# Half steps ahead of the first outputs, single weight pieces and a reordered third tile in a fused attention and feed-forward kernel

## The chip, the cores and the metric

One core of one Trainium2 chip. The metric is the time of one execution on the device in microseconds (us). Runs of a kernel are called fast or slow: slow is a run more than 1.5% above the fastest of the same kernel. Kernels that are compared were run in turns on one chip, with the kernel before among them.

## The reference, cut to what matters

Lightning attention with a decaying state (4 batches, 8 heads, 768 positions, head width 64), then a gated feed-forward block over its 3072 tokens (width 512, inner width 1536).

```python
for b in range(nb):                               # 12 blocks of 64 positions
    intra = (einsum('bhic,bhjc->bhij', qb, kb) * Dmask) @ vb
    inter = (qb * lam_pow) @ kv_state
    out[:, :, sl] = intra + inter
    kv_state = lam_block * kv_state + (kb * rev_pow)^T @ vb
...
x = attn_out.transpose(0, 2, 1, 3).reshape(3072, 512)
g = x @ w_gate
out = (g * sigmoid(g) * (x @ w_val)) @ w_out
```

## The kernel before

The work is cut into 12 attention groups (two blocks of 128 positions each) and six feed-forward tiles of 512 tokens; tile t needs groups 2t and 2t+1. Everything is issued in one hand-made order: each `step(t, fc)` is one of the 12 slices of tile t's inner width (four gate and four value matmuls), and `at(step, fn, ...)` hangs other work behind a step.

Weights come as fp32 in pieces of one or two columns of 128, are cast to bf16 on ScalarE (gate) and GpSimd (value), and share raw buffers and SyncE's queue with q, k and v:

```python
def w_piece(c0, c1, eng=None):
    cs = slice(c0 * 128, c1 * 128)
    n = (c1 - c0) * 128
    if n == 128:
        both = raw_pool.tile([128, 2, MC, n], FP32, name="wraw", tag="raw")
    for j, (w_sb, w_d) in enumerate(((wg_sb, wg_d), (wv_sb, wv_d))):
        t = both[:, j] if n == 128 else raw_pool.tile([128, MC, n], FP32, name="wraw", tag="raw")
        (eng or nc.sync).dma_start(out=t, in_=w_d[:, :, cs])   # rows of n floats
        w_raw.append((w_sb[:, :, cs], t))
...
w_piece(0, 1); w_piece(1, 2); w_piece(2, 4); w_piece(4, 6)
```

A piece of two columns has rows of 1024 bytes in memory, a single one rows of 512. Groups from 3 on are transposed by a DMA, which `cast_scaled` issues behind its two casts; from group 6 on the casts are spread over the third tile (t = 2):

```python
def cast_scaled(g, eng=nc.vector):
    nc.scalar.copy(out=<k half of qk>, in_=kraw)
    eng.tensor_tensor(out=<q half of qk>, in0=qraw, in1=qfac(g), op=ALU.mult)
    dma_transpose(g)                              # on SyncE's queue
...
    at(s1b[11], ffn_out, 0, 0)                    # first output block
    at(s1b[11], ahead, 5)
    at(s1b[11], run_later, 3)
    at(s1b[11], ffn_out, 0, 1)
    at(s1b[11], core_a, 5)
    at(s1b[11], ffn_out, 0, 2)
    at(s1b[11], core_b, 5)
    at(s1b[11], cast_scaled, 6)                   # group 6's casts and transpose
    at(s1b[11], load_group, 7)
    at(s1b[11], v_scale, 6, nc.gpsimd)
    at(s1b[11], ffn_out, 0, 3)
```

Of the kernel before, what the change touches and what calls it, by code (L numbers as in the profile page):

```python
# [9 lines left out]
BF16 = mybir.dt.bfloat16  # L10
# [27 lines left out]
def _body(ctx, tc, nc, q, k, v, lam, moe_w_gate, moe_w_val, moe_w_out, out):  # L38
    B, H, S, D = q.shape
    HP = H // 2  # L40
    BLK = 128
# [3 lines left out]
    MC = DM // 128  # L45
    FC = DFF // 128
    NG = NBLK * B // 2
    M = BLK // 2
# [20 lines left out]
    xt_pool = ctx.enter_context(tc.tile_pool(name="xt", bufs=2))  # L69
    h_pool = ctx.enter_context(tc.tile_pool(name="h", bufs=2))  # L70
    sil_pool = ctx.enter_context(tc.tile_pool(name="sil", bufs=3))
# [7 lines left out]
    def bank():  # L79
        b = banks[ring[0] % 8]  # L80
        ring[0] += 1
        return b
# [44 lines left out]
    def warm_up(n, cols=512):  # L127
        b = bank()
        for _ in range(n):
            nc.tensor.matmul(b[:, 0:cols], warm[:, 0:128], warm[:, 0:cols], start=True, stop=True)  # L130
# [29 lines left out]

    lam_ps = bank()
    warm_up(4)
    nc.tensor.matmul(lam_ps[:, 0:H], ones[:, 0:128], lam_row, start=True, stop=True)
    warm_up(3)
    def warm_into(b, n, cols=256):
# [354 lines left out]
    def ffn_val(t, fc, b0=0, b1=B):  # L520
        if ("h", t) not in st:
            st[("h", t)] = h_pool.tile([128, FC, B, BLK], BF16, name="h", tag="h")
        h_sb, xt, sil = st[("h", t)], st[("xt", t)], st[("sil", t, fc, b0)]
        N = (b1 - b0) * BLK
        fs = slice(fc * 128, fc * 128 + 128)
        vp = bank()
        for mc in range(MC):
            nc.tensor.matmul(vp[:, 0:N], wv_sb[:, mc, fs],  # L528
                             xt[:, b0 // 2:b1 // 2, mc].rearrange("p g b n -> p g (b n)"),
                             start=(mc == 0), stop=(mc == MC - 1))  # L530
        nc.vector.tensor_tensor(out=h_sb[:, fc, b0:b1].rearrange("p b n -> p (b n)"),  # L531
                                in0=sil[:, 0:N], in1=vp[:, 0:N], op=ALU.mult)
# [5 lines left out]
    def ffn_out(t, b, last=False):  # L538
        h_sb = st[("h", t)]
        osb = osb_pool.tile([128, DM], FP32, name="osb", tag="osb")  # L540
        row = groups[2 * t + b // 2][0] * S + (groups[2 * t + b // 2][1] * 2 + b % 2) * BLK
        halves = ((0, DM // 2, nc.scalar.copy, nc.scalar), (DM // 2, DM, nc.vector.tensor_copy, nc.sync)) \
            if last else ((0, DM, nc.scalar.copy, nc.scalar),)
        for c0, c1, fn, eng in halves:
            ps = bank()[:, 0:c1 - c0]
            for fc in range(FC):
                nc.tensor.matmul(ps, h_sb[:, fc, b], wo_sb[:, fc, c0:c1],  # L547
                                 start=(fc == 0), stop=(fc == FC - 1))
            fn(out=osb[:, c0:c1], in_=ps)  # L549
            eng.dma_start(out=bass.AP(tensor=out.tensor, offset=out.offset + row * DM + c0,  # L550
                                      ap=[[DM, 128], [1, c1 - c0]]),
                          in_=osb[:, c0:c1])
# [25 lines left out]
    w_piece(1, 2)  # L578
    w_piece(2, 4)
    w_piece(4, 6)  # L580
    cast_half(0, 0, (None, DVEC))
# [79 lines left out]
    ring[0] = 2  # L661
    ffn_fc(0, 1, 2, 4)
    upd_copy(1, (1,))
    state(0)
# [17 lines left out]
    at(s0[3], load_group, 2, "kq")  # L682
    at(s0[3], w_piece, 10, 12)
    at(s0[3], swapped_q_table)
    at(s0[4], w_cast)
    at(s0[4], state, 1)
    at(s0[4], load_group, 2, "v")
    at(s0[5], load_group, 3)
# [6 lines left out]
    at(s0[8], w_cast)  # L695
    at(s0[8], v_scale, 2, nc.gpsimd)
    at(s0[9], scores, 2)
# [32 lines left out]
    at(s1b[6], wo_cast)  # L730
    at(s1b[6], v_scale, 5, nc.gpsimd)
    at(s1b[8], wo_cast)
    at(s1b[9], core_a, 4)
    at(s1b[10], core_b, 4)
    at(s1b[10], wo_cast, ACTC)
    at(s1b[11], ffn_out, 0, 0)
    at(s1b[11], ahead, 5)
    at(s1b[11], run_later, 3)
    at(s1b[11], ffn_out, 0, 1)
    at(s1b[11], core_a, 5)  # L740
    at(s1b[11], ffn_out, 0, 2)
    at(s1b[11], core_b, 5)
    at(s1b[11], cast_scaled, 6)
    at(s1b[11], load_group, 7)
    at(s1b[11], v_scale, 6, nc.gpsimd)
    at(s1b[11], ffn_out, 0, 3)

    outs = [(1, b) for b in range(4)]
    for t in range(2, NG // 2):
        sn = [step(t, fc) for fc in range(FC)]  # L750
        if t == 2:
            at(sn[2], ahead, 6)
        for j, g in ((3 if t == 2 else 0, 2 * t + 3), (7 if t == 2 else 6, 2 * t + 4)):
            if g < NG:
                at(sn[j], cast_scaled, g)
                if g + 1 < NG:
                    at(sn[j], load_group, g + 1)
                at(sn[1 + j], v_scale, g, nc.gpsimd)
        if t + 1 < NG // 2:
            at(sn[6 if t == 2 else 4], attend, 2 * t + 2)  # L760
            at(sn[10], attend, 2 * t + 3)
        for n, o in zip((0, 3, 7, 9), outs):
            at(sn[n], ffn_out, *o)
        outs = [(t, b) for b in range(4)]
# [41 lines left out]
```

## Time and profile before

| | kernel before |
|---|---|
| time, median of 3 | 228.36 us (228.12 to 229.23) |
| the profiled run | 229.38 us, 1.0 us above that median; span of the profile 227.7 us |
| TensorE busy | 218.2 us, 96% |
| largest wait of TensorE after 15 us | 1.77 us, first output block |

The columns are the stretch in us, its length, the busy time of each engine, the granted clock of TensorE, the mean busy share of the 16 DMA engines, and GB/s:

```profile
16.00:20.00 4.00, 4.00 (x41) 3.29 (x40) 1.82 (x5) 3.54 (x8) 1.81 (x4) 1.00 1.08 379
20.00:24.00 4.00, 4.00 (x20) 1.77 (x19) 1.54 (x3) 2.30 (x5) 3.11 (x7) 1.00 1.09 385
```

The transfer engines are full, and TensorE is full too. Both are at their limit at once. The timeline at 30 us (start, duration, engine, line, what) shows how close the two are:

```profile
30.48 1.18 POOL L273 CAST qk<-qraw 128x512 bf16<-128x512 f32 x2 [1.81 <-DMA qraw<-in_q_dram]
31.56 1.06 PE L289 MATMUL bank<-ident,qk 128*128 128x128 bf16 x16
```

GpSimd waits 1.81 us for group 2's q, casts it in two halves, and TensorE transposes it at 31.56 without a wait: there is no bracket on its line.

### The profile page before, as it was taken

What the parts mean: (1) busy time and instruction counts of PE and PEld (TensorE: products, weight loads), DVE (VectorE), ACT (ScalarE), POOL (GpSimd) and SP (SyncE); (2) the same over time, 40 slices, a digit from 0 to 9 for tenths busy, and PEclk for the clock granted to TensorE, in tenths of its full rate; (3) what the DMA queues carried; (4) which work ended last, traced back from release to release, by engine and by line L of the source; (5) the groups of instructions that cost most, each with busy time, mean ns of one, the idle gap of its engine ahead of it and who ended that gap; (6) DMA issues with size and microseconds to landing.
All of it is one profiled execution on the core that took longest, in us unless ns stands there. A gap on an engine that the chain in (4) does not pass through costs nothing.

```text
span 227.7 us, 5890 instructions
## 1 busy us (share of the span) xinstructions
PE 218.2 (96%) x2431; PEld 118.3 (52%) x2443; DVE 89.5 (39%) x151; ACT 107.2 (47%) x209; POOL 88.9 (39%) x131
## 2 busy tenths in 40 slices
PE   8789999999997999999999999999999999999994
PEld 3556456878853544454544544544544444444443
DVE  2664347685924213545362361353242123222200
ACT  5878585745562446464354363454433423322221
POOL 5676737641595232978373092092160000000000
PEclk9999999999999999999999999999999999999999
DMA  6999999899997879799877748815101101101122
GB/s 201 345 359 382 366 330 325 206 240 285 389 191 179 238 157 217 183 207 192 217 177 184 183 101 200 214 49 138 49 3 48 46 3 46 46 0 46 49 92 92
DMA packets 88012, 39.70 MB, mean 174 GB/s; under 512 B 57650, under 2 KB 83506, under 8 KB 87986
## 3 DMA queue, kind: packets, MB, share of 16 engines
q1 hardware_dynamic: 83474, 32.64, 55.3%
q10 hardware_dynamic: 4512, 6.69, 8.3%
q8 instruction: 19, 0.31, 0.6%
q14 instruction: 7, 0.06, 0.1%
HBM read 28.31 MB, written 6.29 MB: 152 GB/s over the span
## 4 chain that ended last, share of the span: by engine, by line
PE 82%; DMA 5%; SPq 5%; POOL 5%; issue 1%; ACT 0%; DVE 0%; DVEq 0%; POOLq 0%
PE bank L547 26%; PE bank L514 25%; PE bank L528 24%; SPq L99 4%; DMA woraw<-in_moe_w_out_dram 3%; DMA v<-in_v_dram 2%; POOL wo_sb L232 2%; POOL v_s L238 2%; PE bank L474 2%; PE bank L461 2%; PE bank L382 1%; PE bank L352 1%; SPq L227 1%; POOL kvf L421 1%; PE bank L326 0%
## 5 line engine op out<-in xcount | busy, mean ns | idle before, releaser
L531 DVE TENSOR_TENSOR h<-sil,bank 128x512 bf16<-128x512 bf16 (+1 forms) x87 | 51.5, 595 | 108.9 <-PE bank L528 93.2
L514 PE MATMUL bank<-xt,wg_sb 128*128 128x512 bf16 (+1 forms) x348 | 76.6, 343 | 0.0
L528 PE MATMUL bank<-xt,wv_sb 128*128 128x512 bf16 (+1 forms) x348 | 76.4, 342 | 0.0
L547 PE MATMUL bank<-wo_sb,h 128*128 128x512 bf16 (+1 forms) x288 | 64.3, 370 | 2.5 <-POOL wo_sb L232 1.8
L518 ACT ACTIVATE sil<-bank 128x512 bf16<-128x512 f32 (+1 forms) x87 | 45.8, 527 | 44.2 <-PE bank L514 41.2
L528 PEld LDWEIGHTS <-wv_sb 128*128 128x128 bf16 x348 | 34.0, 98 | 28.3
L547 PEld LDWEIGHTS <-h 128*128 128x128 bf16 x300 | 29.1, 98 | 34.3 <-issue 2.0
L514 PEld LDWEIGHTS <-wg_sb 128*128 128x128 bf16 x348 | 32.4, 98 | 27.2 <-DVE xt L486 0.3
L549 ACT COPY osb<-bank 128x512 f32<-128x512 f32 (+1 forms) x24 | 13.9, 578 | 55.4 <-PE bank L547 53.3
L238 POOL TENSOR_TENSOR v_s<-v,dec 128x1024 bf16<-128x1024 f32 (+1 forms) x14 | 23.2, 1667 | 14.4 <-DMA v<-in_v_dram 11.4
L421 POOL TENSOR_TENSOR kvf<-kvs,ups 128x256 f32<-128x256 f32 x8 | 5.8, 727 | 43.5 <-ACT ups L404 42.2
L333 DVE TENSOR_TENSOR ssb<-bank,causal 128x512 bf16<-128x512 f32 x24 | 15.3, 684 | 4.2 <-PE bank L326 4.1
L486 ACT CAST xt<-bank 128x512 bf16<-128x512 f32 x21 | 12.7, 663 | 2.9 <-PE bank L474 2.4
L421 POOL TENSOR_TENSOR kvf<-kvf,ups 128x256 f32<-128x256 f32 x16 | 13.4, 840 | 0.6
L430 POOL CAST kvn<-kvf 64x256 bf16<-64x256 f32 x24 | 11.6, 483 | 1.5
L404 ACT COPY ups<-bank 128x256 f32<-128x256 f32 (+1 forms) x24 | 9.5, 449 | 2.4 <-PE bank L382 1.4
L260 DVE TENSOR_TENSOR qk<-qraw,qdn 128x1024 bf16<-128x1024 f32 x6 | 7.7, 1280 | 4.5 <-DMA qraw<-in_q_dram 4.5
L258 ACT CAST qk<-kraw 128x1024 bf16<-128x1024 f32 x9 | 9.4, 1043 | 0.0
L357 DVE TENSOR_TENSOR ssb<-bank,causaln 128x512 bf16<-128x512 f32 x12 | 8.3, 688 | 1.2 <-PE bank L352 1.1
L232 POOL CAST wo_sb<-woraw 128x1024 bf16<-128x1024 f32 x5 | 5.1, 1040 | 7.3 <-DMA woraw<-in_moe_w_out_dram 7.3
L221 POOL CAST wv_sb<-wraw 128x1024 bf16<-128x1024 f32 (+1 forms) x6 | 5.8, 971 | 5.3 <-DMA wraw<-in_moe_w_val_dram 5.2
L474 PE MATMUL bank<-ssb,v_s 64*64 64x128 bf16 (+1 forms) x384 | 6.9, 208 | 0.5 <-ACT guard L445 0.5
(63 smaller groups left out, 117.2 us busy)
## 6 DMA issues: line engine op xcount, KB each, us to landing
out_dram<-osb ACTq DMA_DIRECT2D x23, 256.0 KB, 2.1
v<-in_v_dram SPq DMA_DIRECT2D x16, 256.0 KB, 4.7
woraw<-in_moe_w_out_dram SPq DMA_DIRECT2D x6, 512.0 KB, 7.4
kraw<-in_k_dram SPq DMA_DIRECT2D x24, 128.0 KB, 3.3
qraw<-in_q_dram SPq DMA_DIRECT2D x24, 128.0 KB, 3.6
wraw<-in_moe_w_gate_dram SPq DMA_DIRECT2D x5, 512.0 KB, 6.8
wraw<-in_moe_w_val_dram SPq DMA_DIRECT2D x5, 512.0 KB, 6.7
kraw<-in_k_dram SPq DMA_DIRECT2D x4, 512.0 KB, 6.9
```

Source lines behind the costliest of these rows:

```text
L238: eng.tensor_tensor(out=st[("vs", g)][:, h0:h1], in0=st[("v", g)][:, h0:h1].rearrange("p h (s d) -> p h s d", s=2), in1=vfac(g, h0, h1), o ...
L333: nc.vector.tensor_tensor(out=ssb[:, h2, 2 * c:2 * c + 2].rearrange("p a s n -> p a (s n)"), in0=sp[(c, h2)].rearrange("p (a x) -> p a x", ...
L421: nc.gpsimd.tensor_tensor(out=o, in0=f, in1=u, op=ALU.add)
L430: nc.gpsimd.tensor_copy(out=o[64 - h2 * 64:128 - h2 * 64], in_=f[h2 * 64:h2 * 64 + 64])
L474: nc.tensor.matmul(op[r][h2 * 64:h2 * 64 + 64, cols(g, hp, s)], v_s[ps, 2 * hp + h2, s], ssb[ps, h2, hp * 2 + s] if g >= NAT0 else ssb[ps, ...
L486: fns[r](out=xt[:, g % 2, :, r].rearrange("p h (m s) -> p h s m", s=2) if g < NAT0 else xt[:, g % 2, :, :, r * M:r * M + M], in_=op[r].rea ...
L514: nc.tensor.matmul(gp[:, 0:N], wg_sb[:, mc, fs], xt[:, b0 // 2:b1 // 2, mc].rearrange("p g b n -> p g (b n)"), start=(mc == 0), stop=(mc = ...
L518: nc.scalar.activation(sil[:, 0:N], gp[:, 0:N], AF.Silu)
L528: nc.tensor.matmul(vp[:, 0:N], wv_sb[:, mc, fs], xt[:, b0 // 2:b1 // 2, mc].rearrange("p g b n -> p g (b n)"), start=(mc == 0), stop=(mc = ...
L531: nc.vector.tensor_tensor(out=h_sb[:, fc, b0:b1].rearrange("p b n -> p (b n)"), in0=sil[:, 0:N], in1=vp[:, 0:N], op=ALU.mult)
L547: nc.tensor.matmul(ps, h_sb[:, fc, b], wo_sb[:, fc, c0:c1], start=(fc == 0), stop=(fc == FC - 1))
L549: fn(out=osb[:, c0:c1], in_=ps)
```

## The change: its intent, and the diff

The intent is to fill TensorE's one wait in the middle by running four half steps (a step over half of the tile's tokens, matmuls of 256 columns) of the third tile ahead of the first output block, with the casts of the output weights reordered; to get the first weights and group 2's v in smaller pieces, so that each can start sooner; to keep the start busy a little longer; and to take group 7's v from GpSimd to VectorE.

```diff
-    h_pool = ctx.enter_context(tc.tile_pool(name="h", bufs=2))
+    h_pool = ctx.enter_context(tc.tile_pool(name="h", bufs=5))    # halves of 6 slices
...
+    b = bank()
+    for n in range(30):
+        r = slice(n % 2 * 64, n % 2 * 64 + 64)
+        nc.tensor.matmul(b[r, 0:8], warm[r, 0:64], warm[r, 0:8], start=True, stop=True, skip_group_check=True)
+    warm_up(2)
+    nc.tensor.matmul(lam_ps[:, 0:H], ones[:, 0:128], lam_row, start=True, stop=True)
     warm_up(4)
-    nc.tensor.matmul(lam_ps[:, 0:H], ones[:, 0:128], lam_row, start=True, stop=True)
-    warm_up(3)
...
-        halves = ((0, DM // 2, ...), (DM // 2, DM, ...)) if last else ...
+        halves = ((0, DM - 128, ...), (DM - 128, DM, ...)) if last else ...
...
-    w_piece(2, 4)
-    w_piece(4, 6)
+    for c in range(2, 6):
+        w_piece(c, c + 1)
...
-    at(s0[3], w_piece, 10, 12)
+    at(s0[3], w_cast)
+    at(s0[3], w_piece, 10, 11)
...
-    at(s0[4], load_group, 2, "v")
+    at(s0[4], load_fp32, 2, nc.sync, v, "v", 0, H // 2)
+    at(s0[4], load_fp32, 2, nc.sync, v, "v", H // 2, H)
+    at(s0[4], w_piece, 11, 12)
...
-    at(s1b[6], v_scale, 5, nc.gpsimd)
     at(s1b[8], wo_cast)
+    at(s1b[8], v_scale, 5, nc.gpsimd)
     at(s1b[9], core_a, 4)
-    at(s1b[10], core_b, 4)
+    at(s1b[10], core_b, 4, SPLIT)
     at(s1b[10], wo_cast, ACTC)
-    at(s1b[11], ffn_out, 0, 0)
...
+    NH = 4
+    s2 = [step(2, fc, 0, 2) for fc in range(NH)][-1]
+    at(s2, ffn_out, 0, 0)
...                                               # the same order as before, behind s2
-        sn = [step(t, fc) for fc in range(FC)]
+        sn = [step(t, fc, 2 if t == 2 and fc < NH else 0) for fc in range(FC)]
...
-                at(sn[1 + j], v_scale, g, nc.gpsimd)
+                at(sn[1 + j], v_scale, g, nc.vector if g == 7 else nc.gpsimd)
```

More of the change, by code (lines that the diff above doesn't have):

```diff
@@ L46, in _body @@
     FC = DFF // 128
+    FH = FC // 2
     NG = NBLK * B // 2
@@ L520, in ffn_val @@
     def ffn_val(t, fc, b0=0, b1=B):
-        if ("h", t) not in st:
-            st[("h", t)] = h_pool.tile([128, FC, B, BLK], BF16, name="h", tag="h")
-        h_sb, xt, sil = st[("h", t)], st[("xt", t)], st[("sil", t, fc, b0)]
+        hn = ("h", t, fc // FH)
+        if hn not in st:
+            st[hn] = h_pool.tile([128, FH, B, BLK], BF16, name="h", tag="h")
+        h_sb, xt, sil = st[hn], st[("xt", t)], st[("sil", t, fc, b0)]
         N = (b1 - b0) * BLK
@@ L530, in ffn_val @@
                              start=(mc == 0), stop=(mc == MC - 1))
-        nc.vector.tensor_tensor(out=h_sb[:, fc, b0:b1].rearrange("p b n -> p (b n)"),
+        nc.vector.tensor_tensor(out=h_sb[:, fc % FH, b0:b1].rearrange("p b n -> p (b n)"),
                                 in0=sil[:, 0:N], in1=vp[:, 0:N], op=ALU.mult)
@@ L538, in ffn_out @@
     def ffn_out(t, b, last=False):
-        h_sb = st[("h", t)]
         osb = osb_pool.tile([128, DM], FP32, name="osb", tag="osb")
         row = groups[2 * t + b // 2][0] * S + (groups[2 * t + b // 2][1] * 2 + b % 2) * BLK
-        halves = ((0, DM // 2, nc.scalar.copy, nc.scalar), (DM // 2, DM, nc.vector.tensor_copy, nc.sync)) \
+        halves = ((0, DM - 128, nc.scalar.copy, nc.scalar), (DM - 128, DM, nc.vector.tensor_copy, nc.sync)) \
             if last else ((0, DM, nc.scalar.copy, nc.scalar),)
@@ L546, in ffn_out @@
             for fc in range(FC):
-                nc.tensor.matmul(ps, h_sb[:, fc, b], wo_sb[:, fc, c0:c1],
+                nc.tensor.matmul(ps, st[("h", t, fc // FH)][:, fc % FH, b], wo_sb[:, fc, c0:c1],
                                  start=(fc == 0), stop=(fc == FC - 1))
@@ L662, in _body @@
     ffn_fc(0, 1, 2, 4)
+    w_cast()
     upd_copy(1, (1,))
@@ L695, in _body @@
     at(s0[8], w_cast)
-    at(s0[8], v_scale, 2, nc.gpsimd)
+    at(s0[8], v_scale, 2, nc.gpsimd, 0, H // 2)
+    at(s0[8], v_scale, 2, nc.gpsimd, H // 2, H)
+    at(s0[9], w_cast)
     at(s0[9], scores, 2)
@@ L730, in _body @@
     at(s1b[6], wo_cast)
-    at(s1b[6], v_scale, 5, nc.gpsimd)
     at(s1b[8], wo_cast)
+    at(s1b[8], v_scale, 5, nc.gpsimd)
     at(s1b[9], core_a, 4)
-    at(s1b[10], core_b, 4)
+    at(s1b[10], core_b, 4, SPLIT)
     at(s1b[10], wo_cast, ACTC)
-    at(s1b[11], ffn_out, 0, 0)
-    at(s1b[11], ahead, 5)
-    at(s1b[11], run_later, 3)
-    at(s1b[11], ffn_out, 0, 1)
-    at(s1b[11], core_a, 5)
-    at(s1b[11], ffn_out, 0, 2)
-    at(s1b[11], core_b, 5)
-    at(s1b[11], cast_scaled, 6)
-    at(s1b[11], load_group, 7)
-    at(s1b[11], v_scale, 6, nc.gpsimd)
-    at(s1b[11], ffn_out, 0, 3)
+    NH = 4
+    s2 = [step(2, fc, 0, 2) for fc in range(NH)][-1]
+    at(s2, ffn_out, 0, 0)
+    at(s2, ahead, 5)
+    at(s2, run_later, 3)
+    at(s2, ffn_out, 0, 1)
+    at(s2, core_a, 5)
+    at(s2, ffn_out, 0, 2)
+    at(s2, core_b, 5)
+    at(s2, cast_scaled, 6)
+    at(s2, load_group, 7)
+    at(s2, v_scale, 6, nc.gpsimd)
+    at(s2, ffn_out, 0, 3)
     outs = [(1, b) for b in range(4)]
     for t in range(2, NG // 2):
-        sn = [step(t, fc) for fc in range(FC)]
+        sn = [step(t, fc, 2 if t == 2 and fc < NH else 0) for fc in range(FC)]
         if t == 2:
-            at(sn[2], ahead, 6)
-        for j, g in ((3 if t == 2 else 0, 2 * t + 3), (7 if t == 2 else 6, 2 * t + 4)):
+            at(sn[4], ahead, 6)
+        for j, g in ((4 if t == 2 else 0, 2 * t + 3), (8 if t == 2 else 6, 2 * t + 4)):
             if g < NG:
@@ L757, in _body @@
                     at(sn[j], load_group, g + 1)
-                at(sn[1 + j], v_scale, g, nc.gpsimd)
+                at(sn[1 + j], v_scale, g, nc.vector if g == 7 else nc.gpsimd)
         if t + 1 < NG // 2:
-            at(sn[6 if t == 2 else 4], attend, 2 * t + 2)
+            at(sn[7 if t == 2 else 4], attend, 2 * t + 2)
             at(sn[10], attend, 2 * t + 3)
-        for n, o in zip((0, 3, 7, 9), outs):
+        for n, o in zip((1, 5, 7, 9) if t == 2 else (0, 3, 7, 9), outs):
             at(sn[n], ffn_out, *o)
```

## The prediction

> **What bounds the kernel now**
>
> I read the busy shares first, then the chain of work that ended last, then the timeline around every idle gap of the TensorE that a listing by engine shows, and last the DMA issues.
>
> ```profile
> PE 218.2 (96%) x2431; PEld 118.3 (52%) x2443; DVE 89.5 (39%) x151; ACT 107.2 (47%) x209; POOL 88.9 (39%) x131
> PE   8789999999997999999999999999999999999994
> PE 82%; DMA 5%; SPq 5%; POOL 5%; issue 1%; ACT 0%; DVE 0%; DVEq 0%; POOLq 0%
> ```
>
> TensorE is the bound: 96% busy, and 82% of the chain is its own work. The row of 40 slices shows where it is not full: the first three slices (to 17 us, the first loads), the thirteenth (68 to 74 us), and the last. From 15 us to the end of the matmuls at 224.3 us a change can only take away idle time of TensorE; moving matmuls about is worth nothing in itself. The timeline of TensorE alone marks the idle time before each entry; from 15 us on it has three gaps of 0.16 to 0.27 us and this one:
>
> ```profile
> 69.57 1.02 PE L547 MATMUL bank<-wo_sb,h 128*128 128x512 bf16 x4 [1.77 <-POOL wo_sb L232]
> ```
>
> The chain of waits shows what made it:
>
> ```profile
> 61.70 0.70 POOL kvf L421
> 62.85 0.70 POOL kvf L421
> 63.62 0.61 POOL kvs L424
> 64.69 1.97 POOL wo_sb L232 x2
> 66.66 1.87 POOL v_s L238
> 68.54 0.99 POOL wo_sb L232
> 69.57 1.02 PE bank L547 x4
> ```
>
> The first output block (line 547) needs all twelve chunks (128 rows each) of the output weights. GpSimd casts chunks 4 to 7, then spends 1.87 us scaling group 5's v, and only then casts chunks 8 and 9. TensorE has done eight of its twelve matmuls by 67.8 us and waits until 69.57. Chunks 10 and 11, cast on ScalarE, were ready at 67.9.
>
> Two waits that cost nothing now lie close behind it:
>
> ```profile
> 80.66 1.80 SPq L251 DMA_TRANSPOSE qkt<-qk  x1
> 92.22 1.32 DVE L260 TENSOR_TENSOR qk<-qraw,qdn 128x1024 bf16<-128x1024 f32 x1
> 93.69 2.03 SPq L251 DMA_TRANSPOSE qkt<-qk  x1
> 96.96 1.92 POOL L238 TENSOR_TENSOR v_s<-v,dec 128x1024 bf16<-128x1024 f32 x1
> 98.93 0.44 PE L382 MATMUL bank<-v_s,qk 64*64 64x64 bf16 x32
> 99.20 0.50 PE L352 MATMUL bank<-qkt 64*64 64x64 bf16 x32
> ```
>
> These belong to groups 6 and 7. Group 6's transpose is issued at 80.66, group 7's loads stand behind it in SyncE's queue, group 7's q lands at 92.0, VectorE scales it, group 7's transpose goes out at 93.69 and takes 4.9 us to land, at 98.6. Its first reader (line 352) runs at 99.20: 0.6 us of slack. GpSimd's scaling of group 7's v ends at 98.88, 0.05 us before its reader (line 382). So the third tile is already fed just in time.
>
> **What the Trainium skill says**
>
> "TensorE: Matmul & The Clock Gate", section "Back-to-back issue gap", puts a warm matmul at N/2.4 + 2.5 ns, so 216 ns for 512 columns and 109 ns for 256. The trace agrees: in the chain twelve matmuls of 512 columns take 2.59 us (216 each), four of 512 take 0.86, four of 256 take 0.44. Halving a step therefore costs almost nothing.
>
> "GPSIMD Engine Reference", section "Elementwise — side-by-side cycle accounting", has a two-input operation about 1.96 times slower on GpSimd. Here the ratio is smaller, 1914 ns (v, line 238) against 1280 ns (q, line 260, the same shape on VectorE): 1.5.
>
> "SBUF — State Buffer", section "SBUF: two separate sides", says that a VectorE operation with two SBUF inputs and a GpSimd operation hold their shared port pair exclusively, and the later one blocks. The trace agrees: the GpSimd add that begins at 92.42, beside VectorE's q scaling, takes 1.70 us where its neighbours take 0.72.
>
> **The change part by part**
>
> 1. Half steps of the third tile (tile 2) ahead of the first outputs, with five half-size h buffers. Four half steps, each 4 gate and 4 value matmuls of 256 columns, 2 x 0.436 = 0.87 us: 3.49 us of work that comes before the first output block instead of after it. They need only group 4's x. Splitting its two evacuations over VectorE and ScalarE makes it ready at about 65.9 instead of 66.5, when the last half step of tile 1 ends (65.9). TensorE then reaches the first output block at 69.4. The cast order changes too: three weight casts before v, so chunks 8 and 9 are ready at 64.63 + 3 x 1.02 = 67.7. The wait is thus removed from both sides: the casts come earlier and TensorE comes later. Sum: -1.77. The halving adds some 0.01 us per group, 16 groups: +0.15. The fifth h buffer lets the half steps be written before the outputs release tile 0's.
>
> 2. The delay this makes. Group 5's attention, which stands between the output blocks, now comes 3.49 - 1.77 = 1.7 us later. ScalarE evacuates it and only then casts group 6's k, so group 6's transpose goes out at about 82.4 instead of 80.66. Group 7's loads follow it in the same queue: q lands at about 93.7, VectorE is done at 95.0, the transpose goes out at 95.2 and lands, with 4.5 to 4.9 us, at 99.7 to 100.1. TensorE's place for its reader: before the attention of group 6 the change puts eight steps instead of seven (+1.73) and removes 1.77 of wait, so still at about 99.2. That is a new wait of 0.5 to 0.9 us. Group 8 inherits the delay: its transpose landed at 110.4, reader at about 112.8, slack 2.4 us. There TensorE is 1.7 us earlier less the new wait, the transpose about 1.5 later: from -0.1 to +0.3. Sum, an estimate: +0.7.
>
> 3. Group 7's v on VectorE, 1.28 us instead of 1.92 on GpSimd. Its state additions on GpSimd begin 1.7 us later (they follow group 6's update), would end at about 98.7, and v behind them at 100.6: TensorE would have waited 1.5 us at line 382. On VectorE it can begin when it lands (about 95.4) and after the mask before it, 96.5, and ends by 97.8, ahead of 98.9. So this part gains nothing against the kernel before; it prevents a loss that part 1 would make. VectorE delays two products of h by about 2 us, which eight banks and three buffers for the gate absorb. Sum: 0.
>
> 4. Weight columns 0 to 5 in single pieces, group 2's v in halves ahead of column 11. No TensorE gap between 15 and 38 us is over 0.25 us, so nothing waits there for weights; two GpSimd casts of 617 ns replace one of 1042. Group 2's v scaling ended at 36.68, its reader began at 36.73: that wait is 0.1 us, and with attention's small gaps around it gives -0.1 to -0.2. Sum: -0.1.
>
> 5. Start: 30 tiny matmuls and two warm-ups before the decay row, instead of four warm-ups. Four took 1.86 us; thirty at 15 to 40 ns plus two is 1.3 to 2.0. ScalarE's logarithm began at 3.27 and its table load ended at 3.12, so at most 0.15 us. What bounds the start is the loads, group 1's v landing at 11.3, which do not change. Sum: -0.05.
>
> 6. Tail: the last block split 384 and 128 instead of 256 and 256. TensorE's sum is the same, 12 x (162 + 56) against 24 x 109. VectorE's copy shrinks from 424 ns (256 columns) towards 290, by the slope from 688 ns at 512; the last transfer halves to 64 KB. Sum: -0.2.
>
> Together: -1.77 + 0.15 + 0.7 - 0.1 - 0.05 - 0.2 = -1.27, so 227.1 us. I shade this to 226.9, because the positions of attention and casts in tile 2 look chosen to keep part 2's wait small, and my landing times move in a block where they might compress.
>
> **The rivals**
>
> (a) No new wait: the loads behind group 6's transpose catch up, and the whole 1.77 stays. For it: DMA moved only 9 GB/s at 80 to 82 us, so the queue is empty when the transpose goes out. Against it: the eight loads have 0.65 us each of issue time, serial, and that does not shrink. It gives 226.2.
>
> (b) The wait only moves: group 7's late transpose plus group 8's take back all of the 1.77. For it: every station of that chain is just in time, and loads of 64 by 64 pieces took 8 to 9 us from first issue to last landing. Against it: 0.6 and 2.4 us of slack must first be used up. It gives 228.0 to 228.4.
>
> (c) VectorE becomes the bound around 92 to 98 us: q, v and four masks of 0.69 us stand ahead of h products there, and its two-input operations block GpSimd's state additions, about 1 us each. If group 6's last state part comes after 98.6, TensorE waits. By my count it is ready at 96.8, or 97.8 with one more block: close. It would add up to 1 us, 227.9.
>
> **Range and chances**
>
> The sure part is -1.77 - 0.2 + 0.15 = -1.8, the uncertain part 0 to 1.7 of waits given back, and 0.2 each way for the rest. That makes 225.9 to 228.2 the range that should hold it 8 times in 10, with 226.9 as the prediction. 2% is 4.6 us; no idle time of that size exists after 15 us, and nothing above adds that much. So 0.03 faster, 0.95 within 2%, 0.02 slower.
>
> **What would show it right or wrong**
>
> Right: the gap before line 547's first block is gone and no GpSimd entry stands in the chain at 61 to 69 us; group 6's transpose is issued at 82 or later; a TensorE wait of 0.3 to 1 us stands before line 352's or its successor's scores of group 7, ended by the transpose; VectorE's v scaling ends before the update of group 7; the last copy takes about 0.3 us. Wrong: a gap remains at the first outputs (then ScalarE's cast or bank reuse holds the half steps), the start shifts by over 0.3 us, or TensorE waits for VectorE or GpSimd in tile 2 instead of the transpose.

## The result, and the profile after

| | before | after |
|---|---|---|
| time, median of 5 | 228.36 us | 231.71 us (230.24 to 236.39) |
| ratio of fast runs | | 1.0115, 95% interval 1.0065 to 1.0164 |
| span of the profile | 227.7 us | 228.5 us |

The kernel got slower by about 1%, where the prediction said 0.6% faster: still within 2%, but outside of its range. One of the five runs was slow (236.39 us, clock 0.985). Ratios are the mean time of one kernel's fast runs over that of the other's of the same rounds, so not quite the ratio of the medians quoted.

Busy time of the engines and the chain that ended last, after:

```profile
PE 220.5 (96%) x2504; PEld 121.8 (53%) x2504; DVE 92.0 (40%) x157; ACT 107.9 (47%) x215; POOL 88.6 (39%) x134
PE 79%; DMA 9%; SPq 7%; DVE 1%; issue 1%; POOL 0%; ACT 0%; DVEq 0%
```

POOL has left the chain, as meant, but the share of the transfers and of SyncE's queue went up from 5% and 5% to 9% and 7%. The list of TensorE's waits says where (line, what it waited for, total us, times, longest):

```profile
PE bank L294 <- POOL qk L278: 0.9, 1, 0.9
PE bank L519 <- ACT wg_sb L226: 0.5, 1, 0.5
PE bank L357 <- DMA qkt<-qk: 0.5, 1, 0.5
PE bank L534 <- POOL wv_sb L226: 0.4, 1, 0.4
```

The wait for the output weights is gone. Four took its place, three of them for weights and for group 2's q, before 34 us. Their origin is in the transfers of the start:

```profile
16.00:20.00 4.00, 4.00 (x37) 3.18 (x34) 1.63 (x4) 3.28 (x9) 1.54 (x4) 1.00 0.98 280
20.00:24.00 4.00, 4.00 (x20) 1.79 (x19) 1.38 (x2) 2.95 (x7) 2.79 (x5) 1.00 0.99 282
```

280 GB/s in place of 380, with the 16 engines still 98% busy: they aren't idle, they get less done. (The share counts overlapping packets, so it can pass 1.) Group 2's q lands at 32.8 us in place of 30.4, and the cast that began at 30.48 begins at 32.88:

```profile
32.88 0.62 POOL L278 CAST qk<-qraw 128x512 bf16<-128x512 f32 x1 [1.94 <-DMA qraw<-in_q_dram]
33.55 0.62 PE L294 MATMUL bank<-ident,qk 128*128 128x128 bf16 x8 [0.94 <-POOL qk L278]
```

In the third tile, group 6's and 7's transposes go out later than before (80.66 and 93.69 there), and TensorE waits for group 7's, as the prediction said:

```profile
84.66 1.92 SPq L256 DMA_TRANSPOSE qkt<-qk  x1
97.26 1.62 SPq L256 DMA_TRANSPOSE qkt<-qk  x1
102.15 0.45 PE L357 MATMUL bank<-qkt 64*64 64x64 bf16 x32 [0.47 <-DMA qkt<-qk]
```

### The profile page after: what moved, and what is told of

It is laid out like the page before. It is cut to its first block, busy times and chain, and to the rows that moved or that the text cites.

```text
span 228.5 us, 6054 instructions
## 1 busy us (share of the span) xinstructions
PE 220.5 (96%) x2504; PEld 121.8 (53%) x2504; DVE 92.0 (40%) x157; ACT 107.9 (47%) x215; POOL 88.6 (39%) x134
## 4 chain that ended last, share of the span: by engine, by line
PE 79%; DMA 9%; SPq 7%; DVE 1%; issue 1%; POOL 0%; ACT 0%; DVEq 0%
PE bank L552 26%; PE bank L519 23%; PE bank L534 23%; SPq L218 4%; DMA qraw<-in_q_dram 4%; SPq L100 3%; DMA wraw<-in_moe_w_val_dram 2%; DMA qkt<-qk 2%; PE bank L479 2%; PE bank L466 2%; PE bank L387 1%; DVE ssb L338 1%; PE bank L331 1%; DMA out_dram<-osb 1%; PE bank L357 1%
## 5 line engine op out<-in xcount | busy, mean ns | idle before, releaser
L523 ACT ACTIVATE sil<-bank 128x512 bf16<-128x512 f32 (+1 forms) x91 | 46.2, 511 | 41.4 <-PE bank L519 38.9
L552 PE MATMUL bank<-wo_sb,h 128*128 128x512 bf16 (+2 forms) x300 | 65.7, 371 | 0.0
L534 PEld LDWEIGHTS <-wv_sb 128*128 128x128 bf16 x364 | 35.4, 98 | 27.5 <-POOL wv_sb L226 0.9
L519 PEld LDWEIGHTS <-wg_sb 128*128 128x128 bf16 x364 | 33.8, 98 | 27.0 <-ACT wg_sb L226 1.0
L552 PEld LDWEIGHTS <-h 128*128 128x128 bf16 x300 | 28.6, 98 | 32.5
L243 POOL TENSOR_TENSOR v_s<-v,dec 128x1024 bf16<-128x1024 f32 (+1 forms) x14 | 21.5, 1544 | 16.8 <-DMA v<-in_v_dram 13.8
L491 ACT CAST xt<-bank 128x512 bf16<-128x512 f32 x20 | 12.2, 659 | 3.1 <-PE bank L479 2.7
L426 POOL TENSOR_TENSOR kvf<-kvf,ups 128x256 f32<-128x256 f32 x16 | 12.5, 778 | 0.6
L226 POOL CAST wv_sb<-wraw 128x512 bf16<-128x512 f32 (+1 forms) x9 | 6.4, 711 | 6.1 <-DMA wraw<-in_moe_w_val_dram 6.0
```

Source lines behind the costliest of these rows:

```text
L243: eng.tensor_tensor(out=st[("vs", g)][:, h0:h1], in0=st[("v", g)][:, h0:h1].rearrange("p h (s d) -> p h s d", s=2), in1=vfac(g, h0, h1), o ...
L426: nc.gpsimd.tensor_tensor(out=o, in0=f, in1=u, op=ALU.add)
L491: fns[r](out=xt[:, g % 2, :, r].rearrange("p h (m s) -> p h s m", s=2) if g < NAT0 else xt[:, g % 2, :, :, r * M:r * M + M], in_=op[r].rea ...
L519: nc.tensor.matmul(gp[:, 0:N], wg_sb[:, mc, fs], xt[:, b0 // 2:b1 // 2, mc].rearrange("p g b n -> p g (b n)"), start=(mc == 0), stop=(mc = ...
L523: nc.scalar.activation(sil[:, 0:N], gp[:, 0:N], AF.Silu)
L534: nc.tensor.matmul(vp[:, 0:N], wv_sb[:, mc, fs], xt[:, b0 // 2:b1 // 2, mc].rearrange("p g b n -> p g (b n)"), start=(mc == 0), stop=(mc = ...
```

## The experiments

The expectations use letters. P: single pieces are fetched more slowly. W, in the first four: the new start lets TensorE's clock rise later or fall back (in `e8_cast6_early`, W is another rival). W2: the longer start makes TensorE fetch its instructions earlier, and a stall of SyncE's issue comes with that. L: the first-output wait of the kernel before took up lateness from the start, which the changed kernel pays in full. T: the third tile's waits come from group 6's casts standing too late. C: such waits let TensorE's clock fall to half for a while. Rivals are told with each.

### One part at a time

The first four undo or do the two parts at the start. `e1_pieces_back` is the changed kernel with pairs and a whole v of group 2 again; `e2_only_pieces` is the kernel before with these pieces alone:

```diff
-    w_piece(2, 4)
-    w_piece(4, 6)
+    for c in range(2, 6):
+        w_piece(c, c + 1)
...  (and columns 10 and 11 apart, group 2's v in halves between them)
```

`e3_warm_back` is the changed kernel with the old start, `e4_only_warm` the kernel before with the new one (the diff's first matmuls).

> The changed kernel with weight columns 2 to 5 and 10 to 11 fetched in pairs again, and group 2's v whole and after them. Theory P (the single pieces are fetched more slowly, 280 instead of 380 GB/s from 16 to 24 us, so that the weights of columns 6 to 9 and group 2's k and q come 2 to 2.4 us late and TensorE waits): 226.5 to 227.2 us, no TensorE gap of over 0.3 us between 15 and 36 us, DMA at 360 GB/s or more from 16 to 24 us. Theory W (the new warm-up makes TensorE's clock rise later or fall back in some runs): still 230 to 232 us with a spread of over 2 us between runs. Theory T (the third tile lost it): also 230 or more.

> The kernel before with only the single weight pieces and group 2's v in halves ahead of column 11. Theory P: 230.3 to 232 us, with TensorE gaps of 1.5 to 2.5 us in all between 24 and 34 us. Theory W or T: 228.0 to 228.6, as before.

> The changed kernel with the old warm-up (four wide matmuls, the decay row, three wide). Theory P: no change against the changed kernel, 230 to 231.7 us, unless part of the spread is the clock. Theory W: 227 to 228.5 us, the runs within 1 us of each other, clocks at 0.998 or more.

> The kernel before with only the new warm-up. Theory P: 228.1 to 228.7 us, as before. Theory W: 230 us or more in some runs, with clocks under 0.997 there, and a spread of over 2 us.

| run | median us | ratio (95%) | group 2's q lands | GB/s at 16 to 20, 20 to 24 us | largest wait of TensorE |
|---|---|---|---|---|---|
| e1_pieces_back | 228.73 | 0.9997 (0.9945 to 1.0049) | 31.64 | 311, 376 | 1.00, group 7's transpose |
| e2_only_pieces | 229.97 | 1.0037 (0.9991 to 1.0083) | 32.80 | 262, 262 | 1.11 at 14.4; 1.01, first output |
| e3_warm_back | 229.97 | 1.0041 (0.9991 to 1.0090) | 32.41 | 268, 277 | 1.08, group 7's transpose |
| e4_only_warm | 229.34 | 1.0022 (0.9969 to 1.0076) | 31.39 | 317, 378 | 0.90, first output |

Where the pieces are single, 16 to 24 us moves 262 to 282 GB/s and q comes at 32.4 or later; where they are pairs, it does not. The new start delays q by about 1 us on its own. With pairs again, `e1_pieces_back` is at the time of the kernel before, though not at the 226.5 to 227.2 us that P expected. W fails: with the old start, `e3_warm_back` still takes 229.97 us, where W had 227 to 228.5. Two of six runs of `e4_only_warm` had the low clock that W expected (0.993), but so had three of eleven of the kernel before on this chip (0.990 to 0.993).

In the kernel before, 2.4 us of later loads cost 0.4% (0.8 us), and 1 us costs 0.2%, both within their intervals. P had expected waits of TensorE between 24 and 34 us in `e2_only_pieces`; there are none. Its profile is a poor witness: the clock was at half from 16.2 to 19.6 us, so that TensorE was itself late and came to the first outputs' wait 2.2 us later than in the kernel before (70.02 against 67.80), where GpSimd's cast ended 1.5 us later as well. The stretch has a mean clock of 0.57:

```profile
16.00:20.00 4.00, 4.00 (x52) 2.62 (x41) 1.16 (x2) 1.51 (x4) 1.72 (x3) 0.57 0.91 262
```

The last column of the table suggested L: the first-output wait, 1.77 us in the profile before, is 1.01 and 0.90 here, as if what comes late at the start were taken off this wait. That is read from two profiles, and the next runs speak against it.

The next four repeat both kernels on another chip, undo both parts of the start at once, and ask what about the pieces is slow:

> Control: the kernel before, unchanged, for its own profile on the chip of this batch and for its spread. All theories: ratio 1.00, runs between 228 and 231.7 us. Theory L (TensorE's place is set by load times: group 2's q at 30 to 33 us, the output weights at 67 us, group 7's transpose at 98 to 102 us): the wait at the first outputs plus the waits between 24 and 40 us come to 1.8 to 2.3 us in all in every profile, one growing as the other shrinks. If instead the wait at 69 us is 1.77 us whatever happens before, L falls.

> Control: the changed kernel, unchanged, on the same chip as the others. If the first measurement stands: ratio 1.008 to 1.016, and a profile with TensorE waits of 1.5 to 2.5 us between 24 and 34 us. If the first measurement was largely the luck of its runs: ratio 1.000 to 1.006.

> The changed kernel with the pieces in pairs, group 2's v whole, and the old warm-up: only the third tile's half steps, its casts and v, and the tail are left of the change. My prediction's sum for these parts: 227.0 to 227.6 us where the kernel before has 228.4, ratio 0.994 to 0.997, with a wait of 0.5 to 1 us before group 7's scores. Theory W2 (the new warm-up itself delays the loads): this is faster than the one with pieces back and the new warm-up by 0.5 us or more, and q of group 2 lands at 30.5 us against 31.6 there. If the warm-up is neutral: within 0.3 us of it.

> The kernel before with columns 2 to 5 still in pairs (1 KB rows) but each tensor's pair fetched by two transfers of 256 KB instead of one of 512 KB. It tells why single pieces are slow. If the number of transfers and the few that may be in flight bound it: 16 to 24 us at 260 to 290 GB/s, group 2's q at 32 us or later, 229 to 230 us as with the single pieces alone. If the 512 B rows do: 360 GB/s or more, q at 30.5 to 31.5, no change against the kernel before.

`c1_before_again`: 228.86 us, ratio 1.0027 (1.0001 to 1.0053): the same kernel differs by up to 0.5% from itself, so a smaller difference counts for little unless waits in the traces back it. It was also the test of L, which asked that the first-output wait and the waits between 24 and 40 us sum to 1.8 to 2.3 us in every profile. They sum to 1.50 us here and to 0.92 in `e7_pairs_in_halves`, which is as fast as the kernel before. The test failed. What the two profiles show is that the first-output wait differs between executions with nothing late at the start (`c1_before_again`, then `e7_pairs_in_halves`):

```profile
68.99 1.02 PE L547 MATMUL bank<-wo_sb,h 128*128 128x512 bf16 x4 [1.25 <-POOL wo_sb L232]
68.34 1.02 PE L549 MATMUL bank<-wo_sb,h 128*128 128x512 bf16 x4 [0.42 <-POOL wo_sb L234]
```

The profiled runs took 229.38 us (before), 228.81 and 227.93; less the waits of 1.77, 1.25 and 0.42, 227.6, 227.6 and 227.5 are left. GpSimd's work up to its last cast is the same unbroken chain in all three. It begins at 61.66, 61.10 and 60.44 us, behind two casts of output weights that waited for their loads. So the 1.77 us were read from a run 1.0 us slower than the median. An estimate of the wait in the median run is 228.36 - 227.5, some 0.9 us.

`c2_after_again`: ratio 1.0073 (1.0038 to 1.0108) for its four fast runs, but two of six were slow, at 236.1 and 234.63 us and a clock of 0.993.

`e7_pairs_in_halves` keeps the rows of 1024 bytes of the kernel before and doubles the number of transfers:

```diff
-            (eng or nc.sync).dma_start(out=t, in_=w_d[:, :, cs])
+            ms = [(0, MC)] if n == 128 or c0 not in (2, 4) else [(0, MC // 2), (MC // 2, MC)]
+            for m0, m1 in ms:
+                (eng or nc.sync).dma_start(out=t[:, m0:m1], in_=w_d[:, m0:m1, cs])
```

It took 228.18 us, ratio 0.9999 (0.9967 to 1.0031), and its transfers lost nothing:

```profile
16.00:20.00 4.00, 4.00 (x40) 3.06 (x34) 1.71 (x5) 3.57 (x8) 1.68 (x3) 1.00 1.08 375
20.00:24.00 4.00, 4.00 (x19) 1.78 (x19) 1.38 (x2) 2.42 (x4) 3.15 (x7) 1.00 1.09 385
```

So not the number of transfers, nor their size of 256 KB, but the row. The packets of the trace between 15 and 24 us say the same: one of 1024 bytes takes 46 ns on its engine (median), one of 512 bytes 27. Half the bytes in 0.59 of the time: 16 x 512 / 28.8 (the mean) is 284 GB/s, and 16 x 1024 / 46.2 is 355, which with the busy shares of 0.99 and 1.08 gives the 282 and 383 that the stretches show.

`e5_both_back` is only the third tile's parts and the tail of the change. If the start were all of the loss, it would be the good kernel. It isn't: 227.91 and 228.82 us in its two fast runs, 231.67 to 234.15 in four others, three of those at a clock of 0.993 or less. Its waits in the fast profile are 0.36 us for group 7's v and this one for group 7's transpose:

```profile
100.79 0.45 PE L353 MATMUL bank<-qkt 64*64 64x64 bf16 x32 [1.08 <-DMA qkt<-qk]
```

So the third tile has a trouble of its own.

### The third tile

`c2_after_again` was profiled in a slow run, which points to it; a slow run alone proves nothing, and the test is `e8_cast6_early` below. TensorE's waits, then the clock (the last three columns of the stretches are clock, DMA share, GB/s):

```profile
103.60 0.45 PE L357 MATMUL bank<-qkt 64*64 64x64 bf16 x32 [1.05 <-DMA qkt<-qk]
116.14 0.44 PE L387 MATMUL bank<-v_s,qk 64*64 64x64 bf16 x24 [0.96 <-POOL v_s L243]
118.25 0.45 PE L357 MATMUL bank<-qkt 64*64 64x64 bf16 x32 [1.67 <-DMA qkt<-qk]
```

```profile
97.00:119.00 22.00, 18.32 (x320) 9.26 (x319) 9.51 (x13) 9.00 (x17) 14.87 (x22) 1.00 0.75 180
119.00:122.50 3.50, 3.50 (x9) 1.23 (x10) 0.43 (x1) 1.67 (x3) 2.59 (x5) 0.51 0.75 167
```

3.7 us of waits in the third tile, and less than 1 us behind the last two of them (2.6 us within 4) the clock is at half for 3.4 us, which costs another 1.7. One such window in 230 us gives a mean clock of 1 - 0.5 x 3.4 / 230 = 0.993, the very number of the slow runs; two give 0.985. So the slow runs of the changed kernels may be self-made. If so, and if T holds, moving group 6's casts forward must remove both. `e8_cast6_early` is `e5_both_back` with this edit:

```diff
+    at(s2, cast_scaled, 6)
+    at(s2, load_group, 7)
     at(s2, ffn_out, 0, 2)
     at(s2, core_b, 5)
-    at(s2, cast_scaled, 6)
-    at(s2, load_group, 7)
     at(s2, v_scale, 6, nc.gpsimd)
```

> The changed kernel with its weight pieces, group 2's v and its start as in the kernel before (as e5_both_back), and in addition group 6's q and k casts and the loads of group 7 issued ahead of the third output block and of core_b of group 5, not behind them. Theory T (the new waits in tile 2 come from group 6's transposes, and with them group 7's, starting late): group 6's transpose is issued about 3 us earlier than the 82.2 us of e5_both_back, group 7's about 2 us or more earlier than 97.0, the 1.08 us wait of TensorE before group 7's scores shrinks below 0.4 us, runs at a full clock come out at 226.5 to 227.8 us, and fewer than 2 of 6 runs fall to a clock of 0.993 or below (e5_both_back: 3 of 6). Rival W (the waits come from contention on the transfer path whatever the order is): the wait stays at 0.8 us or more and the clock falls as often. Rival B (what is moved ahead delays VectorE's work for group 5): a new wait of about 1 us on TensorE at the attention of group 5 or at the output block behind it, time as e5_both_back's good runs, 228 to 229.

It took 227.46 us, ratio 0.9949 (0.9921 to 0.9977), all six runs fast with a clock of 0.998 or more (one, at 229.08 us, above the 226.5 to 227.8 expected). TensorE has no wait over 0.27 us after 15 us. Run again on a third chip as `f5_cast6_early_again`, it gave 227.6 us and 0.9962 (0.9940 to 0.9985), again six fast runs. In `f5_cast6_early_again` the transposes of groups 6 and 7 go out at:

```profile
77.85 1.67 SPq L252 DMA_TRANSPOSE qkt<-qk  x1
93.08 1.65 SPq L252 DMA_TRANSPOSE qkt<-qk  x1
```

That is 4.3 and 3.9 us ahead of `e5_both_back` (82.19 and 97.00). T holds for the waits, and rivals W and B fall. In time, `e5_both_back` has only two fast runs to compare with, but this kernel beats the kernel before, and so the changed one too.

> e8_cast6_early again, beside the next two on one chip: ratio 0.993 to 0.997 to the kernel before, 227.3 to 228.0 us, no run at a clock of 0.993 or less. If its gain was chance, the ratio is 0.999 or more.

The prediction gave group 7's v on VectorE a sum of zero, because it prevents a loss of 1.5 us. `e6_v7_pool` (on `e5_both_back`) and `f2_cast6_early_v7_pool` (on `e8_cast6_early`) put it back:

```diff
-                at(sn[1 + j], v_scale, g, nc.vector if g == 7 else nc.gpsimd)
+                at(sn[1 + j], v_scale, g, nc.gpsimd)
```

> e5_both_back with group 7's v scaled on GpSimd as in the kernel before. The prediction says that VectorE saves about 1.5 us of loss here: then TensorE waits 1.0 to 2.5 us more for group 7's state update (the scaled v on GpSimd), and the time is 1 to 2.5 us above e5_both_back's runs at a full clock (227.9 to 228.8), 229 to 231. Rival: GpSimd is free early enough, no wait of 0.5 us or more is named for group 7's v, and the time is as e5_both_back's; then this part of the change wasn't needed.

> e8_cast6_early with group 7's v scaled on GpSimd. In e6_v7_pool, where the casts come late, TensorE waited 1.48 us for this v. If that wait comes from GpSimd's own order (its work for group 6 lies ahead, and moves little), 0.8 to 1.5 us of it stays and the runs come out at 228.2 to 229.2, ratio 0.998 to 1.002, with some at a clock of 0.993 if the wait joins others. If it comes from the late casts through the load of v (moved ahead here with group 7's loads), the wait falls below 0.3 us and the time is e8's, 227.3 to 227.9: then VectorE's part of the change isn't needed either.

`e6_v7_pool`: 230.47 us, ratio 1.0062 (1.0023 to 1.0102), and a wait of 1.48 us. `f2_cast6_early_v7_pool`: 228.88 us, 1.0010 (0.9982 to 1.0038), and this is its wait, with GpSimd's work ahead of it:

```profile
98.44 0.40 POOL L426 CAST kv<-kvs 128x256 bf16<-128x256 f32 x1
98.80 1.91 POOL L239 TENSOR_TENSOR v_s<-v,dec 128x1024 bf16<-128x1024 f32 x1
100.76 0.45 PE L383 MATMUL bank<-v_s,qk 64*64 64x64 bf16 x32 [1.49 <-POOL v_s L239]
```

GpSimd goes from group 6's state straight to this v: the wait comes from its own order, not from the late casts, and VectorE's part is worth 1.5 us of wait. In time it is 1.1 us: 1.0010 against the 0.9962 of `f5_cast6_early_again`, on one chip in two calls.

`e10_cast_order_only` asks whether the half steps are needed at all: the kernel before with the casts reordered, group 4's evacuation split, and the new tail.

```diff
-    at(s1b[6], v_scale, 5, nc.gpsimd)
     at(s1b[8], wo_cast)
+    at(s1b[8], v_scale, 5, nc.gpsimd)
...
-    at(s1b[10], core_b, 4)
+    at(s1b[10], core_b, 4, SPLIT)
```

> The kernel before with only the order of casts changed: group 5's v scaled behind the third cast of the output weights, group 4's core_b split over two engines, and the last output block divided 384 and 128. No half steps. If the first-output wait (1.77 us in the profile before, 1.25 in c1_before_again) is a matter of the order on GpSimd, it falls to 0.3 us or less and the time to 227.0 to 227.8 us, ratio 0.993 to 0.997; then the half steps weren't needed for it. If the half steps are what hides it, the wait stays at 1.0 us or more, with the time at 228.2 to 228.8. If a wait taken away there only returns in tile 2 (rival b of the prediction), the first-output wait is gone and there are 1 us or more of new waits in 75 to 125 us.

228.20 us, ratio 0.9975 (0.9936 to 1.0013). GpSimd's cast is no longer waited for, but other things are:

```profile
69.48 0.59 PE L547 MATMUL bank<-wo_sb,h 128*128 128x512 bf16 x2 [0.53 <-ACT wo_sb L232]
70.23 0.45 PE L382 MATMUL bank<-v_s,qk 64*64 64x64 bf16 x32 [0.16 <-POOL v_s L238]
71.84 0.64 PE L326 MATMUL bank<-qkt 64*64 64x128 bf16 x32 [1.16 <-DMA qkt<-qk]
```

Neither of the expected outcomes: in this profile the wait moved, but only 2 us on, to group 5's transpose, which lands at 71.8. The three waits sum to 1.85 us. The half steps, 3.5 us of work, would carry TensorE beyond them. But the profiled run was the slowest of the six (230.23 us; the fastest took 227.08), and in time the kernel without half steps isn't told apart from `e8_cast6_early` (0.9975 against 0.9949, with overlapping intervals). Whether the half steps are needed is not shown.

### Why the longer start costs

W2 says that it is the number of instructions. `e13_tiny_later` adds the 30 tiny matmuls behind the old warm-up and changes nothing else:

```diff
     warm_up(3)
+    b = bank()
+    for n in range(30):
+        r = slice(n % 2 * 64, n % 2 * 64 + 64)
+        nc.tensor.matmul(b[r, 0:8], warm[r, 0:64], warm[r, 0:8], start=True, stop=True, skip_group_check=True)
```

> The kernel before with the 30 tiny matmuls added behind the old warm-up, so that TensorE has some 60 more instructions at its start, while the old warm-up stays as it was. Theory W2 (more instructions at the start move TensorE's second fetch of instructions forward, and SyncE's issue of transfers stalls for about 2 us together with it): the second fetch of TensorE's instructions begins at 11.4 to 11.8 us (12.1 to 12.5 in the kernel before), SyncE's stall begins at about 11.4, and group 2's q lands at 31.2 to 31.8 us (30.3 to 30.6 in the kernel before), as in e4_only_warm. Rival (the order of the warm-up itself or the clock does it, or chance): the fetch and group 2's q stay where the kernel before has them. Time within 0.5% of before either way.

The second block of TensorE's instructions (16 KB, on a queue of its own in the trace that is taken to be TensorE's) was fetched at 11.60 us (kernels with the old start: 12.2 to 12.5, but 13.27 in `e2_only_pieces`, whose long issue of SyncE came late too, at 12.88), and SyncE's issue that is long came earlier too. In SyncE's queue, kernel before, then this one:

```profile
11.46 0.69 SPq L213 DMA_DIRECT2D wraw<-in_moe_w_gate_dram  x1
12.20 1.82 SPq L213 DMA_DIRECT2D wraw<-in_moe_w_val_dram  x1
```

```profile
10.70 0.69 SPq L217 DMA_DIRECT2D wraw<-in_moe_w_val_dram  x1
11.44 1.90 SPq L217 DMA_DIRECT2D wraw<-in_moe_w_gate_dram  x1
```

Group 2's q landed at 31.73. All three are as W2 says, though that the fetch causes the long issue is inferred from their moving together. The time, 230.41 us and 1.0060 (1.0024 to 1.0096), was more than the half per cent expected, from four runs. Why an earlier stall of the same length makes the stretch from 16 to 20 us slower (325 GB/s, 379 before) stays open.

### Do the parts add up?

`f1_after_cast6_early` is the whole changed kernel with only the edit of `e8_cast6_early`. `f3_cast6_early_pieces` and `f4_cast6_early_warm` put the pieces and the start, each alone, on `f5_cast6_early_again`, which has no first-output wait left.

> The whole changed kernel with one thing moved: group 6's casts and group 7's loads ahead of the third output block and of group 5's core_b, as in e8_cast6_early. If the loss has two parts that add (late loads at the start, 2.4 us; waits in the third tile and the clock that falls behind them), this takes only the second away: the wait before group 7's scores falls below 0.3 us, no run has a clock of 0.993 or less, and the runs lie at 229.0 to 230.2 us, ratio 1.002 to 1.007. If the third tile's waits are all of the loss, it comes to e8's time, 227.3 to 227.8, ratio 0.995. If they are none of it, it stays at 230.2 to 231.5, ratio 1.007 or more, with slow runs as before.

> f5_cast6_early_again with the changed kernel's single weight pieces and halves of group 2's v. Theory P with L (single pieces are fetched slower, and with the first-output wait gone nothing takes the delay up any more): group 2's q lands at 32.3 to 33.0 us instead of 30.3, 16 to 24 us moves 260 to 290 GB/s, and the runs lie 1.7 to 2.5 us above f5's, ratio to before 1.002 to 1.006. In e2_only_pieces, where the first-output wait was still there to take it up, the same part cost only 0.4%. Prediction's step 4 (nothing waits there for weights): within 0.3 us of f5's.

> f5_cast6_early_again with the changed kernel's longer start (30 tiny and 6 larger matmuls). Theory W2: the second fetch of TensorE's instructions comes at 11.5 to 11.9 us, group 2's q lands at 31.3 to 31.7 us, TensorE waits 0.2 to 0.7 us for it at about 31.8, and the runs lie 0.3 to 1.1 us above f5's. Prediction's step 5 (the start gains 0.05 us): within 0.3 us of f5's, no wait there.

| run | median us | ratio to before (95%) | mean of fast runs less f5's |
|---|---|---|---|
| f5_cast6_early_again | 227.60 | 0.9962 (0.9940 to 0.9985) | 0 |
| f3_cast6_early_pieces | 229.37 | 1.0038 (1.0012 to 1.0064) | +1.8 us |
| f4_cast6_early_warm | 228.37 | 0.9989 (0.9967 to 1.0011) | +0.6 us |
| f1_after_cast6_early (both) | 230.44 | 1.0063 (1.0024 to 1.0101) | +2.5 us (same chip). It was run at another time. |

1.8 + 0.6 = 2.4, and both together cost 2.5, with some 0.9 us of uncertainty in the last. The pieces cost 0.4% in the kernel before and 0.8% here; the start cost 0.2% there and 0.3% here. With these intervals neither pair is told apart, so L, which needs the losses to be larger here, isn't shown in time either. What `f3_cast6_early_pieces` shows is where the pieces make TensorE wait:

```profile
28.21 1.04 PE L530 MATMUL bank<-xt,wv_sb 128*128 128x512 bf16 x4 [0.83 <-POOL wv_sb L222]
33.46 1.18 PE L290 MATMUL bank<-ident,qk 128*128 128x128 bf16 x16 [0.76 <-POOL qk L274]
```

0.83 + 0.76 = 1.6 of the 1.8 us. The expectation for `f4_cast6_early_warm` was right in size; its wait came elsewhere than expected, at a weight:

```profile
20.87 1.04 PE L534 MATMUL bank<-xt,wv_sb 128*128 128x512 bf16 x4 [0.77 <-POOL wv_sb L226]
```

And `f1_after_cast6_early` had six fast runs with clocks of 0.998 or more, while the changed kernel had three slow runs in eleven. Its ratio, 1.0063, isn't told apart from the changed kernel's 1.0073 and 1.0115. They were run at other times. So what the third tile's waits cost in the fast runs of the whole change is not shown.

About C: kernels with the half steps and the late casts (after, c2, e1, e3, e5, e6) had a clock of 0.993 or less in 11 of 35 runs, those with early casts (e8, f1 to f5) in 1 of 36. On one chip (15), the late casts fell in 8 of 18 runs and `e8_cast6_early` in none of six. That and two profiles speak for it: the one above, and `e2_only_pieces`, where the half clock follows a wait of 1.11 us. It isn't fully shown: the late and the early casts otherwise ran on different chips, `e2_only_pieces` and `e4_only_warm` fell in 4 of 12 runs without any half steps, one wait of 1.5 us alone (f2) never brought the clock down, one run of e5 was slow at a full clock, and the kernel before fell to 0.993 in 4 of 61 runs too, for reasons of its start or of the chip.

## Why the prediction was wrong

By the ratio of fast runs the change cost 2.6 us, where the prediction had a gain of 1.5: it failed by about 4 us. Its own sums for the range (-1.8, 0 to 1.7, 0.2 each way) give 226.4 to 228.5 and not 225.9 to 228.2; neither holds the result.

**Step 1, half steps and casts (-1.77): the wait is gone as said, but the term was about twice too large.** It was read from a run 1.0 us above the median, and the same wait was 1.25 and 0.42 us in other profiles. `e8_cast6_early` and `f5_cast6_early_again`, without this wait and without the new ones, gain 1.2 and 0.9 us by their ratios, where the terms -1.77, +0.15 and -0.2 (tail) sum to -1.8. Which half of the step did it, the half steps or the order of the casts, stays open after `e10_cast_order_only`.

**Step 2, new waits in the third tile (+0.7): right in mechanism, too small.** Group 6's transpose was predicted at 82.4 and went out at 82.19 in `e5_both_back`. Group 7's q was predicted to land at 93.7 and landed at about 95.6; its transpose was predicted at 95.2 and went out at 97.00. The wait is 1.08 and not 0.5 to 0.9. In about a third of the runs of the kernels with late casts the clock falls, and the slow runs take 3 to 6 us longer, which no term of the sum held; that the waits cause this is not shown.

**Step 3, v on VectorE (0, prevents 1.5): right in size.** Taken back, it costs a wait of 1.48 or 1.49 us. Its timing was not: VectorE's v was to end by 97.8 and ended at 99.2 in `e5_both_back`, and TensorE waited 0.36 us for it.

**Step 4, single pieces (-0.1): this step failed most.** Its words were "nothing waits there for weights", read from TensorE having no gap over 0.25 us between 15 and 38 us. The transfers in that stretch were at their limit and group 2's q came just in time; single pieces, with rows of 512 bytes, take a quarter off the rate. +1.8 us.

**Step 5, start (-0.05): this failed too.** The 30 matmuls were counted by their 15 to 40 ns on TensorE, which was right (0.96 us for all) and harmless; the sum with two warm-ups is 1.4 to 2.1 us and not 1.3 to 2.0. But with their 60 instructions the instruction fetch comes earlier, and SyncE's long issue with it. +0.6 us, small beside the noise, but `e13_tiny_later`, with these instructions alone, lost 0.6% too.

**Step 6, tail (-0.2)** wasn't measured alone. The last copy takes 0.29 us, as predicted, and the span ends 3.1 us after its start in `e8_cast6_early`, where it was 3.3 before.

With steps 4 and 5 taken out and the casts in place, the kernel runs at 227.5 us. The prediction's terms for what is left (-1.77, +0.15, -0.2) would give 226.5; by the estimate above, most of the missing 1 us is step 1's.

## What to carry to other kernels

An engine without gaps isn't an engine with slack: ask for each input how long it was there before its reader, and if the answer is zero, a change that slows its transfer is on the critical path. A wait read from one profile is that execution's: compare the profiled run's time with the median, or read several profiles, before taking the wait for its full worth. When work is put in front of a block, move the casts and loads that hang behind the block forward with it, or the next tiles starve.

## What the Trainium skill lacked or had wrong

- The Trainium skill, "DMA: Bandwidth & Descriptors", section "Specifications", has 512 bytes and more as the size for line rate. Here packets of 512 bytes took 27 ns and packets of 1024 bytes 46 ns, so 512 still loses: 262 to 288 GB/s in the stretches of 16 to 24 us of e2, e3 and f3, against 375 to 385 with pairs (before, `e7_pairs_in_halves`). Further down, the page does speak of a fixed cost per packet; it is this row that misleads.
- The Trainium skill, "Runtime: NRT & Kernel Launch", section "Instruction fetch mechanics", says that crossing a 16 KiB boundary of instructions is mostly hidden. Here SyncE's issue took 1.8 to 2.1 us in place of 0.69 just when TensorE's second block was fetched (before, c1, after, e4, e13; 1.69 in f5 and 1.30 in f1), and 60 more TensorE instructions moved both by 0.7 to 0.8 us (`e13_tiny_later`). That the fetch causes the stall is inferred from their moving together.
- The Trainium skill, "TensorE: Matmul & The Clock Gate", section "HAM oscillation — how this bites in real kernels", has the clock fall after idle gaps of more than about 3.4 us. Here it was at half (0.51 in the stretch) for 3.4 us behind waits of 0.96 and 1.67 us within 4 us (`c2_after_again`), and for 3.4 us behind a wait of 1.11 us (`e2_only_pieces`), none of them near 3.4.
